# The last 64 rows of a first product: from stacked 128-row matmuls to pairs of 64-row matmuls

## The chip, the cores and the metric

The kernel runs on one core of a Trainium2 chip (trn2). The metric is device time in microseconds (us); the time before is the median of three runs. The engines that matter here are TensorE (PE for its matmuls, PEld for its weight loads), VectorE (DVE), ScalarE (ACT), GpSimd (POOL) and the DMA queue that SyncE issues (SP).

## The reference: what is computed

Input `x` is 8 x 4096 x 192, `weight_gen` is 8 x 4096 x 8 x 7; the weights `w_in` (192 x 2048) and `w_out` (2048 x 192) come as float64.

```python
w = softmax(weight_gen, axis=-1)                       # 7 taps per head
out[s, h] = sum over k of w[s, h, k] * x_pad[s + k, h]  # causal, 8 heads of 24 columns
h = out.reshape(32768, 192) @ w_in                     # first product, 192 rows deep
g = h * cos(h)
y = g @ w_out                                          # second product, 2048 rows deep
```

The result is 32768 x 192 in float32.

## The kernel before

**Tiling.** A block is 512 tokens (4 rows on each of 128 partitions); there are 64 blocks. In each block the 2048 columns of h are worked in 16 chunks of 128, two chunks at a time: 8 pairs per block, 512 pairs in all. The main loop (line 436) runs over the pairs; iteration i does the first product of pair i, the cosine chain of pair i and of pair i - 1, and the second product of a piece that lies 6 pairs back. Each engine issues in the order of the program, which is fixed at the end by lines 474 to 483.

**Precision.** Products that have to be as good as float32 are made of two parts, hi and lo, in the type float32r. Weights are split by `two_parts` (line 101), the tokens by `transposed` (line 253), which turns the mixed rows on TensorE (line 257) and splits them on ScalarE (`hi`, line 264) and VectorE (`lo`, line 265).

**First product, `ffn_in` (lines 274 to 284).** The product is 192 rows deep: 128 rows (the a parts) and the last 64 (the b parts). For each chunk five matmuls of 128 rows and 512 tokens are added up in one PSUM bank:

- wa_hi with a_lo, wa_lo with a_hi, wa_hi with a_hi for the 128 rows;
- wb with b_lo, wb with b_hi for the last 64. The tile `wb` holds the hi part of the 64 weight rows in partitions 0 to 63 and the lo part in 64 to 127, and b_hi and b_lo hold the same 64 rows of tokens twice, once in each half. So one matmul gives w_hi * b + w_lo * b, and the two give all four partial products.

That is ten matmuls for a pair, each with its own weights. The tile `h` is two PSUM banks, one for each chunk; there are three such tiles. A pair's h goes ACT `turn` (line 292), DVE fraction (296), ACT sine (300), DVE `g` (303), ACT `ghi` (309), DVE `glo` (313); after that its `h` tile is free for pair i + 3.

**Second product, `ffn_out` (lines 318 to 355).** Eight matmuls of 384 columns in float32r (line 329), then eight of 192 columns in bfloat16 (line 332), then ACT evicts (335).

So TensorE's sequence in most iterations is: ten matmuls of line 282, eight of line 329, eight of line 332, and round again. At pairs 5 and 6 of a block four transposes (line 257) come between lines 282 and 329.

**Preparation of the last 64 weight rows, `w_in_b` (lines 139 to 152).** It loads the raw words of two column ranges into the two halves of a tile, splits them into a temporary tile `parts`, and then copies `parts` into `wb` with four DMAs on the SP queue (line 150), so that hi and lo of one chunk lie one above the other. It is called twice; the first call covers pairs 0, 1, 4 and 5, the second pairs 2, 3, 6 and 7.

**Other work.** POOL mixes the tokens of later blocks (lines 225 to 245). Every four blocks a softmax batch runs, with three steps on DVE (lines 179, 188 to 189, 191).

Of the kernel before, what the change touches and what calls it, by code (L numbers as in the profile page):

```python
# [11 lines left out]
F32 = mybir.dt.float32  # L12
F32R = mybir.dt.float32r
I32 = mybir.dt.int32
# [6 lines left out]
P = 128  # L21
# [7 lines left out]
    return float(v)  # L29


# sin(SIN_SCALE * f + SIN_BIAS) = cos(2 pi f) for -3/4 <= f <= 1/4; both constants are a few ulp
# below 2 pi and pi / 2, so that the argument stays within the table's [-pi, pi].
SIN_SCALE = _below(TWO_PI, 2)
SIN_BIAS = _below(math.pi / 2, 1)

# The upper word of 2.0 ** -127 in float64, read as a float32: smaller values become denormal.
F64_SMALL = float(np.array([2.0 ** -127]).view(np.float32)[1])


# [1 line left out]
def tile_softmax_conv_then_cos_ffn(  # L42
# [8 lines left out]
    nc = tc.nc  # L51

    B, S, D = x.shape
    H, K = weight_gen.shape[2], weight_gen.shape[3]
    G = D // H
    NT = B * S
    F = w_in.shape[1]
    NFC = F // P
    RPP = NT // P          # tokens of one partition, in a row
    R = 4                  # tokens of a partition in one block  # L60
    NB = RPP // R          # blocks
    CT = R * P             # tokens of a block
    PAD = K - 1
    D2 = D - P             # 64
    RW = 16                # tokens of a partition in one softmax batch
    SB = RW // R           # blocks of one softmax batch
    NPAIR = NFC // 2       # pairs of f chunks in a block
    HALF = NPAIR // 2
    LAG = 6                # pairs from the first product to the second
    TR = 5                 # the pair at which the next block is transposed  # L70
    TMP = 6
    CW = 512               # weights of a partition that are converted at once

    const = ctx.enter_context(tc.tile_pool(name="const", bufs=1))
    gpool = ctx.enter_context(tc.tile_pool(name="gpool", bufs=9))
# [1 line left out]
    ps_h = ctx.enter_context(tc.tile_pool(name="ps_h", bufs=3, space=bass.MemoryType.PSUM))  # L77
    ps_m = ctx.enter_context(tc.tile_pool(name="ps_m", bufs=2, space=bass.MemoryType.PSUM))

    # partition q * B + n holds the tokens q * RPP.. of batch n  # L80
    x_v = x.rearrange("n (q r) d -> q n (r d)", r=RPP)
    g_v = weight_gen.rearrange("n (q r) h k -> q n (r h k)", r=RPP)
    o_v = out.rearrange("(n q r) d -> q n (r d)", n=B, r=RPP)
# [3 lines left out]
    nc.gpsimd.memset(early, 0.0)  # L87
    make_identity(nc, ident)

# [1 line left out]
    wa_hi = const.tile([P, F], F32R, name="wa_hi")  # L91
    wa_lo = const.tile([P, F], F32R, name="wa_lo")
    wb = const.tile([P, F], F32R, name="wb")   # rows 0-63 the first part, 64-127 the second
    wo = const.tile([P, NFC, 2 * D], F32R, name="wo")
    wo_b = const.tile([P, NFC, D], BF16, name="wo_b")

# [4 lines left out]
    def two_parts(raw, hi, lo, half=None):  # L101
        shape = hi.shape[1:]
        n = math.prod(shape)

        def shaped(t, steps=1):
            t = t.rearrange("p (n s) -> p n s", s=steps)
            return t if len(shape) == 1 else t.rearrange("p (a b) s -> p a b s", b=shape[1])

        low, top = (shaped(raw, 2)[..., k] for k in range(2))
        t1 = work.tile([P, 2, CW], F32, name="t1", tag="turn", bufs=TMP)  # L110
        size, bits = (shaped(t1.bitcast(I32)[:, k, 0:n])[..., 0] for k in range(2))
        nc.scalar.activation(out=size.bitcast(F32), in_=top.bitcast(F32), func=AF.Abs)
        yield
        nc.vector.tensor_scalar(  # L114
            out=size.bitcast(F32), in0=size.bitcast(F32), scalar1=F64_SMALL, scalar2=None, op0=ALU.max)
        yield
        nc.vector.tensor_scalar(
            out=size, in0=size, scalar1=0x07FFFFFF, scalar2=3,
            op0=ALU.bitwise_and, op1=ALU.logical_shift_left)
        yield  # L120
        # sign, exponent and 20 bits of the mantissa
        nc.vector.scalar_tensor_tensor(
            out=size, in0=top, scalar=-0x40000000, in1=size, op0=ALU.bitwise_and, op1=ALU.bitwise_or)
        yield
        # 3 more bits of the mantissa
        nc.vector.scalar_tensor_tensor(
            out=bits, in0=low, scalar=29, in1=size, op0=ALU.logical_shift_right, op1=ALU.bitwise_or)
        nc.scalar.copy(out=hi, in_=bits.bitcast(F32))  # L128
        if half is not None:
            nc.scalar.copy(out=half, in_=bits.bitcast(F32))  # L130
        yield
        nc.gpsimd.tensor_tensor(out=lo, in0=bits.bitcast(F32), in1=hi.bitcast(F32), op=ALU.subtract)  # L132

    def w_in_a(c0, c1):
        raw = words(c1 - c0)
        nc.sync.dma_start(out=raw, in_=w_in[0:P, c0:c1].bitcast(I32))
        return two_parts(raw, wa_hi[:, c0:c1], wa_lo[:, c0:c1])

    def w_in_b(j):
        raw = words(CW)  # L140
        cols = [slice(n * (F // 2) + j * CW, n * (F // 2) + (j + 1) * CW) for n in range(2)]
        for n in range(2):
            nc.sync.dma_start(out=raw[n * D2:(n + 1) * D2], in_=w_in[P:D, cols[n]].bitcast(I32))

        def convert():
            parts = gpool.tile([P, 2, CW], F32R, name="parts", tag="ghi")
            yield from two_parts(raw, parts[:, 0, :], parts[:, 1, :])
            for n in range(2):
                for m in range(2):
                    nc.sync.dma_start(out=wb.bitcast(F32)[m * D2:(m + 1) * D2, cols[n]],  # L150
                                        in_=parts.bitcast(F32)[n * D2:(n + 1) * D2, m, :])
        return convert()

    w_out_v = w_out.rearrange("(c p) d -> p c d", p=P)

# [4 lines left out]
        cs = slice(2 * q, 2 * q + 2)  # L160
        return two_parts(raw, wo[:, cs, 0:D], wo[:, cs, D:2 * D], wo_b[:, cs, :])

# [1 line left out]
    taps, ready = {}, set()  # L164

    def softmax(r0, r1, eng):
# [27 lines left out]
            out=t, in0=t, in1=den.unsqueeze(2).broadcast_to([P, n, K]), op=ALU.mult)  # L194
        ready.update(range(r0 // R, r1 // R))

# [1 line left out]
    rows, mixed = {}, {}  # L198

    def load_rows(b):  # L200
# [13 lines left out]
    def attention(b, eng, ra=0, rb=R, spare=False):  # L214
        xt = rows[b]
        t = taps[b]
        n = rb - ra
        # the columns from D on repeat the last D2, for both halves of the transposed rows
        if b not in mixed:
            xa_ = work.tile([P, R, D + D2], F32, name="xa")  # L220
            mixed[b] = xa_
        xa = mixed[b]

        def product(k, dst):
            eng.tensor_tensor(  # L225
                out=dst.rearrange("p r (h g) -> p r h g", h=H),
                in0=xt[:, k + ra:k + rb, :].rearrange("p r (h g) -> p r h g", h=H),
                in1=t[:, ra:rb, :, k:k + 1].broadcast_to([P, n, H, G]), op=ALU.mult)

        product(0, xa[:, ra:rb, 0:D])  # L230
        yield
        old = None
        for k in range(1, K + 1):
            if k < K:
                if spare:
                    pr = work.tile([P, R, D], F32, name="pr", tag="turn", bufs=TMP)
                else:
                    pr = work.tile([P, R, D], F32, name="pr", bufs=3)
                product(k, pr[:, ra:rb])
                yield  # L240
            if old is not None:
                if k == K:
                    eng.tensor_tensor(out=xa[:, ra:rb, D:], in0=xa[:, ra:rb, P:D],
                                      in1=old[:, ra:rb, P:D], op=ALU.add)
                eng.tensor_tensor(out=xa[:, ra:rb, 0:D], in0=xa[:, ra:rb, 0:D], in1=old[:, ra:rb],  # L245
                                  op=ALU.add)
                yield
            old = pr

# [1 line left out]
    xT = {}  # L251

    def transposed(b, part):
# [14 lines left out]

        return split

# [1 line left out]
    hs, g_parts = {}, {}  # L272

    def ffn_in(i):
        b, pair = divmod(i, NPAIR)
        a_hi, a_lo, b_hi, b_lo = xT[b]
        h = ps_h.tile([P, 2, CT], F32, name="h")
        for n in range(2):
            fs = slice((2 * pair + n) * P, (2 * pair + n + 1) * P)
            prods = ((wa_hi, a_lo), (wa_lo, a_hi), (wb, b_lo), (wb, b_hi), (wa_hi, a_hi))  # L280
            for m, (w, v) in enumerate(prods):
                nc.tensor.matmul(h[:, n, :], lhsT=w[:, fs], rhs=v,  # L282
                                 start=(m == 0), stop=(m == len(prods) - 1))
        hs[i] = h

# [1 line left out]
    turns = {}  # L287

    def act_turns(i):
# [22 lines left out]
        hi, lo = g_parts[i]  # L312
        nc.vector.tensor_tensor(out=lo, in0=hs.pop(i), in1=hi.bitcast(F32), op=ALU.subtract)  # L313

# [1 line left out]
    sums, finals = {}, {}  # L316

    def ffn_out(j):
# [47 lines left out]
            yield  # L366

    mixing = {1}
# [1 line left out]
    def all_of(*steps):  # L370
        steps = list(steps)
        while steps:
# [55 lines left out]
    for _ in range(4):  # L428
        next(bg)
    all_of(a1, b1)  # L430
# [1 line left out]
    N = NB * NPAIR  # L432

    sm = sm2
    no_split = split = lambda: None
    for i in range(N + LAG):
        b, pair = divmod(i, NPAIR)
# [33 lines left out]
            if (b if pair <= TR + 1 else b + 1) + 3 not in mixing:  # L471
                next(bg, None)

    # each engine issues in the order of this program
    issued = {}
    for ins in nc.cur_bb.bb.instructions:
        if ins.engine in issued:
# [11 lines left out]


def _as_sent(a):
    """float64 has no type on the chip: its words are sent as they are."""
    a = np.ascontiguousarray(a)
    return a.view(np.int64) if a.dtype == np.float64 else a

# [18 lines left out]
```

## Time and profile before

| | us |
|---|---|
| median of three runs | 2418.97 |
| lowest and highest of the three | 2418.47 and 2419.04 |
| span of the profiled execution, first to last instruction | 2416.5 |
| PE busy | 2345.7 |
| PEld busy | 2019.7 |
| DVE busy | 2037.1 |
| ACT busy | 1848.9 |
| POOL busy | 1877.6 |

The profile gives no time for its execution beyond the span; the span is 2.5 us below the median of the runs. Start times in the timeline count from the span's start. Matmuls overlap each other in the pipeline, so the time that one more matmul takes is read from the distance of two starts and not from the duration of one. In a timeline row the columns are start, duration, engine, line, operation, output and inputs, then rows x columns of the array for a matmul, the shape, and the number of merged instructions; a bracket gives the idle time before it and what ended it. The mean granted TensorE clock of the execution is 0.992 of full speed.

### The profile page before, as it was taken

To read this page: it belongs to the slowest core of one execution; us is meant where nothing else is said; L and a number is where in the kernel's file an instruction comes from. 1 tells how busy PE (TensorE), PEld (TensorE's weight loads), DVE (VectorE), ACT (ScalarE), POOL (GpSimd) and SP (SyncE) were. 2 spreads that over 40 slices of the span, in tenths; PEclk is the share of its full clock that TensorE was granted. 3 is DMA by queue.
4 is the path that set the end of the run, shared out by engine and by line. 5 is a ranking of instruction groups with operands and counts; after the bars stand their busy time and mean duration, and the time that the engine had idled before them with its cause. 6 is when DMAs were issued, how large, how long until landed. Compare 5 with 4: busy or idle time off the path is not lost.

```text
span 2416.5 us, 34582 instructions
## 1 busy us (share of the span) xinstructions
PE 2345.7 (97%) x13824; PEld 2019.7 (84%) x13824; DVE 2037.1 (84%) x1820; ACT 1848.9 (77%) x2266; POOL 1877.6 (78%) x1458
## 2 busy tenths in 40 slices
PE   2799999999999999999999999999999999999999
PEld 1588888888888888888888888888888888888888
DVE  8988888888888888888888888888888888888887
ACT  3678777787877778777787777878777787777876
POOL 6698878797787787787787787877877877887841
PEclk8899999999999999999999999999999999999999
DMA  6211220210211120121211211111111201201100
GB/s 163 53 42 36 47 54 24 54 47 23 54 47 31 46 54 24 47 51 27 54 37 33 54 35 43 47 27 51 46 31 47 54 24 46 54 24 48 30 7 20
DMA packets 25456, 104.93 MB, mean 43 GB/s; under 512 B 2782, under 2 KB 5462, under 8 KB 25294
## 3 DMA queue, kind: packets, MB, share of 16 engines
q1 hardware_dynamic: 25294, 102.72, 17.1%
q8 instruction: 108, 1.77, 0.3%
q14 instruction: 54, 0.44, 0.1%
HBM read 76.50 MB, written 25.17 MB: 42 GB/s over the span
## 4 chain that ended last, share of the span: by engine, by line
PE 87%; DVE 6%; ACT 5%; issue 1%; DMA 0%; SPq 0%; ACTq 0%; DVEq 0%
PE h L282 46%; PE ps_m L329 27%; PE ps_m L332 13%; PE ps_m L257 2%; ACT ghi L309 1%; ACT turn L292 1%; DVE h L303 1%; DVE glo L313 1%; DVE den L189 1%; ACT L300 1%; DVE turn L296 1%; ACT turn L300 1%; DVE t L114 1%; ACT L184 1%; DVE den L188 1%
## 5 line engine op out<-in xcount | busy, mean ns | idle before, releaser
L296 DVE TENSOR_TENSOR turn<-h,turn 128x1024 f32<-128x1024 f32 x512 | 625.5, 1222 | 326.3 <-ACT turn L292 323.3
L329 PE MATMUL ps_m<-wo,ghi 128*128 128x384 f32 x4096 | 812.9, 340 | 3.1 <-ACT part L335 3.1
L292 ACT ACTIVATE turn<-h 128x1024 int32<-128x1024 f32 x512 | 524.7, 1025 | 314.3 <-PE h L282 314.3
L329 PEld LDWEIGHTS ps_m<-wo,ghi 128*128 128x128 f32 x4096 | 721.1, 188 | 38.3 <-ACT part L335 3.6
L245 POOL TENSOR_TENSOR xa<-xa,pr 128x768 f32<-128x768 f32 (+1 forms) x384 | 705.4, 1837 | 5.0
L300 ACT ACTIVATE turn<-turn 128x1024 f32<-128x1024 f32 x512 | 543.4, 1061 | 184.2 <-DVE turn L296 184.0
L303 DVE TENSOR_TENSOR h<-h,turn 128x1024 f32<-128x1024 f32 x512 | 629.9, 1230 | 8.3 <-ACT turn L300 8.3
L313 DVE TENSOR_TENSOR glo<-h,ghi 128x1024 bf16<-128x1024 f32 x512 | 621.7, 1214 | 1.1 <-ACT ghi L309 1.1
L225 POOL TENSOR_TENSOR pr<-xt,taps 128x768 f32<-128x768 f32 (+1 forms) x384 | 588.2, 1537 | 0.0
L346 POOL TENSOR_TENSOR part<-part,part 128x384 f32<-128x384 f32 x252 | 256.3, 1017 | 391.2 <-ACT part L335 391.1
L309 ACT CAST ghi<-h 128x1024 fp32r<-128x1024 f32 x512 | 516.3, 1008 | 3.8 <-DVE h L303 2.8
L282 PE MATMUL h<-a_lo,wa_hi 128*128 128x512 f32 x1024 | 454.3, 444 | 33.2 <-DVE glo L313 25.5
L332 PE MATMUL ps_m<-wo_b,glo 128*128 128x192 bf16 x4096 | 426.8, 247 | 0.0
L282 PE MATMUL h<-a_hi,wa_hi 128*128 128x512 f32 x1024 | 408.0, 398 | 0.0
L282 PE MATMUL h<-a_hi,wa_lo 128*128 128x512 f32 x1024 | 406.8, 397 | 1.1 <-POOL wa_lo L132 1.1
L282 PE MATMUL h<-b_hi,wb 128*128 128x512 f32 x1024 | 404.6, 395 | 0.0
L282 PE MATMUL h<-b_lo,wb 128*128 128x512 f32 x1024 | 403.6, 394 | 0.8 <-DVE b_lo L265 0.8
L332 PEld LDWEIGHTS <-glo 128*128 128x128 bf16 x4096 | 311.7, 98 | 82.1 <-issue 82.1
L282 PEld LDWEIGHTS h<-a_lo,wa_hi 128*128 128x128 f32 x1024 | 194.7, 190 | 62.6 <-ACT wa_hi L128 13.6
L335 ACT ACTIVATE part<-ps_m 128x384 f32<-128x384 f32 x512 | 241.4, 472 | 6.8 <-PE ps_m L332 6.8
L282 PEld LDWEIGHTS h<-b_lo,wb 128*128 128x128 f32 x1024 | 194.2, 190 | 48.9 <-DVE b_lo L265 1.3
L282 PEld LDWEIGHTS h<-b_hi,wb 128*128 128x128 f32 x1024 | 194.2, 190 | 45.5
(52 smaller groups left out, 1285.6 us busy)
## 6 DMA issues: line engine op xcount, KB each, us to landing
xt<-in_x_dram SPq DMA_DIRECT2D x62, 960.0 KB, 7.4
out_dram<-fin SPq DMA_DIRECT2D x63, 384.0 KB, 3.9
taps<-in_weight_gen_dram SPq DMA_DIRECT2D x15, 448.0 KB, 8.6
raw<-in_moe_w_out_dram SPq DMA_DIRECT2D x8, 384.0 KB, 3.9
raw<-in_moe_w_in_dram SPq DMA_DIRECT2D x6, 256.0 KB, 6.6
raw<-in_moe_w_in_dram SPq DMA_DIRECT2D x3, 512.0 KB, 5.9
wb<-parts SPq DMA_DIRECT2D x8, 128.0 KB, 4.8
xt<-in_x_dram SPq DMA_DIRECT2D x1, 768.0 KB, 11.7
```

The source lines that it names most:

```text
L225: eng.tensor_tensor(out=dst.rearrange("p r (h g) -> p r h g", h=H), in0=xt[:, k + ra:k + rb, :].rearrange("p r (h g) -> p r h g", h=H), in ...
L245: eng.tensor_tensor(out=xa[:, ra:rb, 0:D], in0=xa[:, ra:rb, 0:D], in1=old[:, ra:rb], op=ALU.add)
L282: nc.tensor.matmul(h[:, n, :], lhsT=w[:, fs], rhs=v, start=(m == 0), stop=(m == len(prods) - 1))
L292: nc.scalar.activation(out=t.bitcast(I32), in_=hs[i], func=AF.Identity, bias=0.25, scale=1.0)
L296: nc.vector.tensor_tensor(out=t, in0=hs[i], in1=t.bitcast(I32), op=ALU.subtract)
L300: nc.scalar.activation(out=t, in_=t, func=AF.Sin, bias=SIN_BIAS, scale=SIN_SCALE)
L303: nc.vector.tensor_tensor(out=hs[i], in0=hs[i], in1=turns.pop(i), op=ALU.mult)
L309: nc.scalar.copy(out=hi, in_=hs[i])
L313: nc.vector.tensor_tensor(out=lo, in0=hs.pop(i), in1=hi.bitcast(F32), op=ALU.subtract)
L329: nc.tensor.matmul(acc[:, 0:2 * D], lhsT=g, rhs=wo[:, fc, :], start=(c == 0), stop=False)
L332: nc.tensor.matmul(acc[:, 0:D], lhsT=g, rhs=wo_b[:, fc, :], start=False, stop=(c == 2 * HALF - 1))
L346: eng.tensor_tensor(out=part, in0=part, in1=old, op=ALU.add)
```

## The change

The last 64 rows are no longer stacked. `wb` is replaced by `wb_hi` and `wb_lo`, each 128 x 1024: partitions 0 to 63 hold the 64 weight rows of the even chunks, partitions 64 to 127 those of the odd ones. In `ffn_in` each pair begins with six matmuls of 64 rows: three products (hi * lo, lo * hi, hi * hi; the product lo * lo is left out), and of each one matmul for the even chunk on partitions 0 to 63 and one for the odd chunk on partitions 64 to 127. They alternate between the halves and write to different PSUM banks. Six matmuls of 128 rows follow for the a parts. A pair has twelve matmuls and twelve weight loads in place of ten and ten.

`w_in_b` loads the raw words of the even chunks into the upper half and of the odd chunks into the lower, in runs of 128 weights (1 KB), and splits them straight into `wb_hi` and `wb_lo`. The temporary tile `parts` and the eight DMAs of line 150 are gone. Its first call now covers pairs 0 to 3 and the second pairs 4 to 7. The rest of the diff takes out comments.

```diff
-    wb = const.tile([P, F], F32R, name="wb")   # rows 0-63 the first part, 64-127 the second
+    wb_hi = const.tile([P, F // 2], F32R, name="wb_hi")
+    wb_lo = const.tile([P, F // 2], F32R, name="wb_lo")
...
+    w_in_odd_even = w_in.rearrange("k (a n c) -> n k a c", n=2, c=P)
+
     def w_in_b(j):
         raw = words(CW)
-        cols = [slice(n * (F // 2) + j * CW, n * (F // 2) + (j + 1) * CW) for n in range(2)]
+        pairs = slice(j * CW // P, (j + 1) * CW // P)
         for n in range(2):
-            nc.sync.dma_start(out=raw[n * D2:(n + 1) * D2], in_=w_in[P:D, cols[n]].bitcast(I32))
-
-        def convert():
-            parts = gpool.tile([P, 2, CW], F32R, name="parts", tag="ghi")
-            yield from two_parts(raw, parts[:, 0, :], parts[:, 1, :])
-            for n in range(2):
-                for m in range(2):
-                    nc.sync.dma_start(out=wb.bitcast(F32)[m * D2:(m + 1) * D2, cols[n]],
-                                        in_=parts.bitcast(F32)[n * D2:(n + 1) * D2, m, :])
-        return convert()
+            nc.sync.dma_start(out=raw[n * D2:(n + 1) * D2].rearrange("k (a c) -> k a c", c=2 * P),
+                              in_=w_in_odd_even[n, P:D, pairs, :].bitcast(I32))
+        cols = slice(j * CW, (j + 1) * CW)
+        return two_parts(raw, wb_hi[:, cols], wb_lo[:, cols])
...
         h = ps_h.tile([P, 2, CT], F32, name="h")
+
+        for m, (w, v) in enumerate(((wb_hi, b_lo), (wb_lo, b_hi), (wb_hi, b_hi))):
+            for n in range(2):
+                rs = slice(n * D2, (n + 1) * D2)
+                nc.tensor.matmul(h[:, n, :], lhsT=w[rs, pair * P:(pair + 1) * P], rhs=v[rs, :],
+                                 start=(m == 0), stop=False)
+
         for n in range(2):
             fs = slice((2 * pair + n) * P, (2 * pair + n + 1) * P)
-            prods = ((wa_hi, a_lo), (wa_lo, a_hi), (wb, b_lo), (wb, b_hi), (wa_hi, a_hi))
-            for m, (w, v) in enumerate(prods):
-                nc.tensor.matmul(h[:, n, :], lhsT=w[:, fs], rhs=v,
-                                 start=(m == 0), stop=(m == len(prods) - 1))
+            for m, (w, v) in enumerate(((wa_hi, a_lo), (wa_lo, a_hi), (wa_hi, a_hi))):
+                nc.tensor.matmul(h[:, n, :], lhsT=w[:, fs], rhs=v, start=False, stop=(m == 2))
         hs[i] = h
```

## The prediction

> **What bounds the kernel now.** I read the page first: busy shares, then the chain that ended last.
>
> ```profile
> span 2416.5 us, 34582 instructions
> ## 1 busy us (share of the span) xinstructions
> PE 2345.7 (97%) x13824; PEld 2019.7 (84%) x13824; DVE 2037.1 (84%) x1820; ACT 1848.9 (77%) x2266; POOL 1877.6 (78%) x1458
> ...
> PE 87%; DVE 6%; ACT 5%; issue 1%; DMA 0%; SPq 0%; ACTq 0%; DVEq 0%
> ```
>
> TensorE carries 87% of the chain. A busy PE need not be a PE at its limit, so I asked for the waits: ACT's first step waits for the h of TensorE, 409 times, while TensorE waits for a free h tile only 17 times.
>
> ```profile
> PE h L282 <- DVE glo L313: 25.5, 17, 6.8
> ...
> ACT turn L292 <- PE h L282: 314.3, 409, 1.4
> ```
>
> The window over four blocks (32 pairs) in the middle gives the rates that the other engines would allow. Its columns are the length, then the busy time of PE, PEld, DVE, ACT and POOL, then the granted clock, the DMA share and GB/s.
>
> ```profile
> 1382.24:1528.50 146.26, 145.52 (x865) 125.68 (x865) 123.67 (x109) 114.35 (x140) 117.19 (x90) 1.00 0.17 42
> ```
>
> A pair takes 146.26 / 32 = 4.57 us. PE idles 0.74 us in the whole window. DVE needs 123.67 / 32 = 3.86 us a pair, so 0.7 us a pair can go before DVE is the bound; ACT and POOL need less. The clock is 1.00. So what a pair costs TensorE is what the kernel costs, and the question is how long the new sequence is. The timeline of one ordinary pair:
>
> ```profile
> 1202.59 0.61 PEld L332 LDWEIGHTS <-glo 128*128 128x128 bf16 x8 [0.16 <-issue]
> 1202.60 0.83 PE L332 MATMUL ps_m<-wo_b,glo 128*128 128x192 bf16 x8
> ...
> 1203.19 0.19 PEld L282 LDWEIGHTS h<-a_lo,wa_hi 128*128 128x128 f32 x1
> 1203.21 0.48 PE L282 MATMUL h<-a_lo,wa_hi 128*128 128x512 f32 x1
> 1203.30 0.19 PEld L282 LDWEIGHTS h<-a_hi,wa_lo 128*128 128x128 f32 x1
> 1203.53 0.39 PE L282 MATMUL h<-a_hi,wa_lo 128*128 128x512 f32 x1
> 1203.53 0.19 PEld L282 LDWEIGHTS h<-b_lo,wb 128*128 128x128 f32 x1
> 1203.76 0.39 PE L282 MATMUL h<-b_lo,wb 128*128 128x512 f32 x1
> ...
> 1205.39 0.40 PE L282 MATMUL h<-a_hi,wa_hi 128*128 128x512 f32 x1
> ...
> 1205.62 1.57 PE L329 MATMUL ps_m<-wo,ghi 128*128 128x384 f32 x8
> ...
> 1207.03 0.83 PE L332 MATMUL ps_m<-wo_b,glo 128*128 128x192 bf16 x8
> ```
>
> Four things are read here. **A matmul of 512 tokens costs 0.2325 us**: from 1203.53 to 1205.39 lie eight steps, 1.86 / 8. Its duration of 0.39 to 0.40 is longer by 0.16, the time that it is still in the pipeline when the next has begun. **Its weights are loaded under the matmul before**: each load starts with that matmul. **A weight load holds the path for 0.11 us**: the loads at 1203.19 and 1203.30 start 0.11 apart though each is shown as 0.19 long. **The turn from line 332 costs little**: the second matmul starts at 1203.53, so the first streams from 1203.53 - 0.2325 = 1203.30, which is when its weights are in; its shown start at 1203.21 is early.
>
> **The change, part by part: TensorE.** Per pair four matmuls of line 282 go, two with b_lo and two with b_hi; the page counts 1024 of each form for the 512 pairs.
>
> ```profile
> L282 PE MATMUL h<-b_hi,wb 128*128 128x512 f32 x1024 | 404.6, 395 | 0.0
> L282 PE MATMUL h<-b_lo,wb 128*128 128x512 f32 x1024 | 403.6, 394 | 0.8 <-DVE b_lo L265 0.8
> ```
>
> Removed: 4 x 0.2325 = 0.93 us a pair. Added: six matmuls of 64 rows and 512 tokens, three on each half. No matmul in the trace has 64 rows, so the second of each two is bounded from both sides: it costs nothing where it runs wholly beside the first, and 0.2325 where it runs after it. From the code the two share no array row, no partition of the moving tile and no PSUM bank. They share the path of the weight loads. For a 64-row load I take the 0.11 of the 128-row one, the nearest row. Two loads, 0.22, fit under one matmul of 0.2325, so from the second product on the two halves can run side by side, with the lower half 0.11 behind the upper. The lag is paid once a pair, where the first two loads come one after the other behind the last matmul of line 332: upper half 1203.30, lower half 1203.41. Three steps from there end at 1203.41 + 3 x 0.2325 = 1204.11; the four matmuls of before would end at 1203.30 + 0.93 = 1204.23. **Saved: 0.12 us a pair, x 512 = 63 us.** The ends are 0.2325 x 512 = 119 saved (no lag) and 2 x 0.2325 x 512 = 238 lost (one after the other).
>
> This assumes that going from 128 rows to 64 and back costs nothing in itself, and the trace has no such turn. The nearest one is between products and transposes:
>
> ```profile
> 1218.69 0.39 PE L282 MATMUL h<-a_hi,wa_hi 128*128 128x512 f32 x1
> 1218.92 0.60 PE L257 MATMUL ps_m<-ident,xa 128*128 128x128 f32 x4
> 1219.27 1.64 PE L329 MATMUL ps_m<-wo,ghi 128*128 128x384 f32 x8
> 1220.76 0.83 PE L332 MATMUL ps_m<-wo_b,glo 128*128 128x192 bf16 x8
> ...
> L257 PE MATMUL ps_m<-ident,xa x512: 270/272/445, 27.6 to 2356.8; 128*128 128x128 f32 x171
> ```
>
> The transposes begin 0.23 after the matmul before, the usual step. They follow each other by (0.60 - 0.27) / 3 = 0.11, which is again one weight load each. From 1218.92 to 1220.76 are 1.84 us: four transposes (0.44) and eight matmuls of line 329 (1207.03 - 1205.62 = 1.41) are 1.85. So a change of operation empties no pipeline here, and I take 0 for the turn too, with 0.16 twice a pair as the other end (the third rival).
>
> **DVE's bursts.** Behind a softmax batch DVE has extra work within six pairs:
>
> ```profile
> 1214.87 1.08 DVE L179 TENSOR_REDUCE top<-taps 128x128 f32<-128x896 f32 x1
> ...
> 1221.64 0.69 DVE L265 SCALAR_TENSOR_TENSOR a_lo<-ps_m,a_hi 128x512 fp32r<-128x512 f32 x1 [0.18 <-ACT a_hi L264]
> ...
> 1227.54 0.69 DVE L265 SCALAR_TENSOR_TENSOR b_lo<-ps_m,b_hi 128x512 fp32r<-128x512 f32 x1 [0.18 <-ACT b_hi L264]
> ...
> 1231.05 1.08 DVE L188 TENSOR_REDUCE den<-taps 128x128 f32<-128x896 f32 x1
> 1232.16 1.53 DVE L189 TENSOR_SCALAR den<-den 128x128 f32<-128x128 f32 x1
> ...
> 1237.09 0.94 DVE L191 RECIPROCAL den<-den 128x128 f32<-128x128 f32 x1
> ```
>
> That is 6.0 us on six pairs, and the 0.74 us of PE idle time in the window belongs to it: PE runs out of h tiles there already. In the burst a faster PE gains nothing more: up to 6 x 0.12 = 0.7 us of the saving is lost each time, 0 if the three h tiles cover it. With some 15 batches that is 0 to 11 us; I take 0.45 each, 7 us.
>
> In later blocks the b parts come first now, which costs nothing: b_lo of the next block is done at 1227.54 + 0.69 = 1228.23, behind pair 6, and is first used at pair 8, a whole pair later.
>
> **The start.** Eight DMAs leave the SP queue:
>
> ```profile
> wb<-parts SPq DMA_DIRECT2D x8, 128.0 KB, 4.8
> ...
> 31.34 0.68 DVE L265 SCALAR_TENSOR_TENSOR b_lo<-ps_m,b_hi 128x512 fp32r<-128x512 f32 x1
> 31.48 0.80 PE L282 MATMUL h<-a_lo,wa_hi 128*128 128x512 f32 x1 [1.98 <-DVE a_lo L265]
> ...
> 40.50 0.79 PE L282 MATMUL h<-a_lo,wa_hi 128*128 128x512 f32 x1 [4.75 <-ACT wa_hi L128]
> ```
>
> Nothing waits for the copies now: the first matmul waited for a_lo and the second pair for wa_hi, so what goes was covered. Afterwards the first matmul needs b_lo, ready at 31.34 + 0.68 = 32.02 in place of 31.48: 0.5 us later. Against that the 64-row matmuls of the second pair need no new wa_hi and fit into the 4.75 us of waiting, worth about a microsecond. The raw words of `w_in_b` come in runs of 1 KB, and a late load would push the conversions behind it; I allow 3 us either way and count 0.
>
> **Sum.** -63 + 7 + 0 = -56 us on the span of 2416.5, which is 2.5 below the median; the same 2.5 lies around it afterwards. 2418.97 - 56 = **2363 us**.
>
> **The rivals.**
>
> *No lag between the halves* (chance 0.10). If the two loads go in together, the whole 119 us are saved, less 6 x 0.2325 = 1.4 us in each of 15 bursts (21): 2418.97 - 98 = 2321. For it: the halves share no row. Against it: the path of the loads is busy 84% of the span and never shows two starts closer than 0.11 in these rows. The Trainium skill, page "TensorE: Matmul & The Clock Gate", section "The mechanism", has packed matmuls of different row groups start about 4 ns apart; by that this rival would hold, and no run here shows it.
>
> *The halves run one after the other* (0.10). Then a pair has two matmuls more: +238, 2657. For it: every matmul of the trace starts one full step after the one before. Against it: none of them could do otherwise, since all use all rows.
>
> *The turn empties the array* (0.25), the one that ends slower. Place: between line 332 and the first 64-row matmul, and again before the first 128-row matmul. Price: what a matmul is still in the pipeline, 0.395 - 0.2325 = 0.16. The last matmul of line 332 ends at 1202.60 + 0.83 = 1203.43; by then the weights of both halves are in (1203.41), so both start at 1203.43, without lag; they stream to 1204.13 and are out at 1204.29, against 1204.23 before: +0.06 x 512 = +31, 2450. It decides from a turn of 0.12: 1203.41 + 0.6975 + 0.12 = 1204.23. Below that the change still gains. Against it: the transposes above. The Trainium skill, page "TensorEngine Tiling (Array Packing)", section "Key Properties", speaks for it: changing the tiling mode drains the engine. No turn of that kind is in the trace, and the page gives no price.
>
> *The turn also holds back the weight loads* (0.10). Then 0.11 for each half come behind 1203.43, the end moves to 1203.65 + 0.6975 + 0.16 = 1204.51, and the weights of the first 128-row matmul add 0.11: 1204.62, +0.39 x 512 = +200, 2619. Against it: the load at 1203.30 starts while line 332 is still in the array.
>
> **How the numbers follow.** Forecast 0.45, the two halves without lag 0.10, the emptying turn 0.25, the turn with loads 0.10, one after the other 0.10. The range of 2310 to 2480 takes in the first three and leaves out the last two, 0.20. The forecast's own range is 2340 to 2390. A measurement of this kernel can tell about 0.2% (4.8 us) from no change. Faster: 0.45 + 0.10 + 0.06 for a turn below 0.12 us; within 0.2%: 0.04, a turn near it; slower: 0.15 + 0.20.
>
> **What would show it.** In the timeline of the changed kernel the rows of 64-row matmuls should come in twos, the second within 0.11 us of the first, and the twos 0.23 apart; a step of 0.23 between all of them shows the halves one after the other. A first 128-row matmul more than 0.24 behind the last 64-row one shows an emptying turn; a weight load that starts only after it shows the last rival. From one group of line 332 to the next an ordinary pair should take 4.31 us in place of 4.43 (line 332 starts at 1202.60 and again at 1207.03). The wait of line 282 for glo should rise from 25.5 us by up to 11. The forecast is wrong if the weight loads of 64 rows take another time than those of 128, or if PE waits for glo in ordinary pairs.

## The result, and the profile after

| | median us | span of the profiled execution | PE clock |
|---|---|---|---|
| before | 2419.01 | 2416.5 | 0.992 |
| after | 2475.72 | 2473.9 | 0.993 |

The change makes the kernel slower: a ratio of 1.0234, 95% interval 1.0219 to 1.0248, 56.7 us. The forecast was 56 us faster. The line numbers shift: the 64-row matmuls are line 280 of the changed kernel, the 128-row ones of the first product line 286, the second product lines 332 and 335.

The page of the changed kernel, busy times and then the chain that ended last:

```profile
span 2473.9 us, 36612 instructions
## 1 busy us (share of the span) xinstructions
PE 2410.1 (97%) x14848; PEld 1888.1 (76%) x14848; DVE 2035.5 (82%) x1820; ACT 1849.6 (75%) x2266; POOL 1878.5 (76%) x1458
...
PE 95%; DVE 3%; ACT 1%; issue 1%; DMA 0%; POOL 0%; SPq 0%; ACTq 0%; DVEq 0%
```

TensorE still bounds it, even more than before: its share of the chain went from 87% to 95%. The busy times of DVE, ACT and POOL moved by less than 2 us; PEld fell by 132 us, though it has 1024 loads more. The window over four blocks, columns as in the prediction:

```profile
1200.00:1349.65 149.65, 149.65 (x929) 117.53 (x930) 123.36 (x109) 114.39 (x140) 117.23 (x90) 1.00 0.17 41
```

Four blocks take 149.65 us in place of 146.26, so 3.39 / 32 = 0.106 us more a pair, 54 us over 512 pairs. PE idles nowhere in this window. The 0.74 us that it waited in DVE's burst is gone: from 200 us on, PE waited for glo 12 times in the kernel before, 8.5 us in all, and once in the changed kernel, 0.5 us. Not every four blocks of the kernel before had such a wait, so 54 is a little less than the 56.7 us measured. So TensorE's own sequence became longer by 0.106 + 0.74 / 32 = 0.13 us a pair. The timeline of one ordinary pair, PE and PEld:

```profile
1202.75 0.61 PEld L335 LDWEIGHTS <-glo 128*128 128x128 bf16 x8 [0.16 <-issue]
1202.76 0.84 PE L335 MATMUL ps_m<-wo_b,glo 128*128 128x192 bf16 x8
1203.52 0.19 PEld L280 LDWEIGHTS h<-b_lo,wb_hi 64*128 64x128 f32 x2 [0.16 <-issue]
1203.52 0.50 PE L280 MATMUL h<-b_lo,wb_hi 64*128 64x512 f32 x2
1203.63 0.19 PEld L280 LDWEIGHTS h<-b_hi,wb_lo 64*128 64x128 f32 x2
...
1203.86 0.39 PE L280 MATMUL h<-b_hi,wb_lo 64*128 64x512 f32 x2
1203.86 0.19 PEld L280 LDWEIGHTS h<-b_hi,wb_hi 64*128 64x128 f32 x2
...
1204.09 0.40 PE L280 MATMUL h<-b_hi,wb_hi 64*128 64x512 f32 x2
1204.41 0.19 PEld L286 LDWEIGHTS h<-a_lo,wa_hi 128*128 128x128 f32 x1 [0.36 <-issue]
1204.42 0.50 PE L286 MATMUL h<-a_lo,wa_hi 128*128 128x512 f32 x1
1204.52 0.19 PEld L286 LDWEIGHTS h<-a_hi,wa_lo 128*128 128x128 f32 x1
1204.75 0.39 PE L286 MATMUL h<-a_hi,wa_lo 128*128 128x512 f32 x1
```

Two things are to be seen. **The 64-row matmuls do run in twos**: a row merges two (x2) and is 0.39 to 0.40 long, no longer than one matmul, and the twos are 0.23 apart. Even their weight loads come in twos, 0.19 for both. **The turns cost time** (a turn is a change between 128-row and 64-row matmuls): no weight load starts while the last 64-row matmuls stream. They start at 1204.09 and stream for 0.2325, to 1204.32; the next load starts at 1204.41, the matmul that needs it streams from 1204.75 - 0.2325 = 1204.52. The load at 1203.86, between 64-row matmuls, starts together with the matmul ahead of it.

That gives the price of each turn:

- **Back to 128 rows:** 1204.52 - 1204.09 = 0.43 where a step is 0.2325, so 0.20. Some 0.09 of it lies between the end of streaming and the load, 0.11 is the load.
- **To 64 rows:** the last matmul of line 335 starts at 1202.76 + 0.84 - 0.25 (its mean duration) = 1203.35, the first 64-row ones stream from 1203.86 - 0.2325 = 1203.63: 0.28, where before it was 1203.30 - 1203.18 = 0.12. So 0.16 more.

Together 0.36 a pair against one step of 0.2325 saved: +0.13, and the pair takes 4.55 us (1207.31 - 1202.76, the next start of line 335) where it took 4.43.

The groups of the 64-row matmuls, with busy time, mean ns and idle time before:

```profile
L280 PE MATMUL h<-b_lo,wb_hi 64*128 64x512 f32 x1024 | 257.5, 500 | 23.0 <-DVE glo L316 19.1 <-DVE b_lo L263 3.9
L280 PE MATMUL h<-b_hi,wb_hi 64*128 64x512 f32 x1024 | 204.7, 396 | 0.0
L280 PE MATMUL h<-b_hi,wb_lo 64*128 64x512 f32 x1024 | 202.0, 391 | 0.0
```

Busy time counts overlapping instructions once: 204.7 / 512 = 0.400 us for two matmuls that last 0.396 each. On the mean of the run the two halves start within 4 ns of each other.

### The profile page after: what moved, and what is told of

The parts are those of the page before. It is cut to its first block, busy times and chain, and to the rows that moved or that the text cites. A ratio compares the mean times of both kernels' runs of the same rounds, so it can differ in the third digit from the quotient of the medians.

```text
span 2473.9 us, 36612 instructions
## 1 busy us (share of the span) xinstructions
PE 2410.1 (97%) x14848; PEld 1888.1 (76%) x14848; DVE 2035.5 (82%) x1820; ACT 1849.6 (75%) x2266; POOL 1878.5 (76%) x1458
## 4 chain that ended last, share of the span: by engine, by line
PE 95%; DVE 3%; ACT 1%; issue 1%; DMA 0%; POOL 0%; SPq 0%; ACTq 0%; DVEq 0%
PE h L286 32%; PE ps_m L332 29%; PE h L280 18%; PE ps_m L335 14%; PE ps_m L255 2%; DVE t L116 1%; DVE glo L316 0%; DVE t L124 0%; DVE h L306 0%; DVE t L128 0%; DVE pr L223 0%; ACT ghi L312 0%; DVE xa L243 0%; DMA raw<-in_moe_w_in_dram 0%; ACT t L114 0%
## 5 line engine op out<-in xcount | busy, mean ns | idle before, releaser
L286 PE MATMUL h<-a_lo,wa_hi 128*128 128x512 f32 x1024 | 461.6, 451 | 3.7 <-ACT wa_hi L130 3.7
L280 PE MATMUL h<-b_lo,wb_hi 64*128 64x512 f32 x1024 | 257.5, 500 | 23.0 <-DVE glo L316 19.1
L286 PEld LDWEIGHTS h<-a_hi,wa_hi 128*128 128x128 f32 x1024 | 194.1, 190 | 46.4
L286 PEld LDWEIGHTS h<-a_hi,wa_lo 128*128 128x128 f32 x1024 | 195.3, 191 | 24.6 <-POOL wa_lo L134 1.8
L280 PE MATMUL h<-b_hi,wb_hi 64*128 64x512 f32 x1024 | 204.7, 396 | 0.0
```

What stands on the lines that cost most here:

```text
L280: nc.tensor.matmul(h[:, n, :], lhsT=w[rs, pair * P:(pair + 1) * P], rhs=v[rs, :], start=(m == 0), stop=False)
L286: nc.tensor.matmul(h[:, n, :], lhsT=w[:, fs], rhs=v, start=False, stop=(m == 2))
```

## The experiments

All are timed against the kernel before, 2419 us. The theory after the result: each turn between 128-row and 64-row matmuls lets the array run empty and holds back the next weights, some 0.2 us each. The main rival: twelve matmuls and twelve loads a pair are too many for TensorE's sequencer, for the profile puts the gaps down to "issue".

**1. Four turns a pair (four_turns).** The edit, on the changed kernel (`pack` and `whole` are its two loops, by product and by chunk):

```diff
-        for m, (w, v) in enumerate(((wb_hi, b_lo), (wb_lo, b_hi), (wb_hi, b_hi))):
...
-        for n in range(2):
-            fs = slice((2 * pair + n) * P, (2 * pair + n + 1) * P)
...
+        pack(0)
+        whole(0, False)
+        pack(1)
+        pack(2, True)
+        whole(1, True)
```

> The same twelve matmuls of a pair, but the 64-row ones are split in two groups (one product, then three 128-row matmuls of the even chunk, then two products, then the odd chunk), so a pair turns between 128 and 64 rows four times and not twice. Theory (each turn empties the array and holds back the next weight loads, about 0.20 us): two more turns a pair, 0.40 x 512 = +205 over the changed kernel, about 2680. Rival (two more instructions of each kind a pair are too many for the sequencer, the turn costs nothing): same instructions, so no change, about 2476. Rival (only the place behind the bfloat16 matmuls is dear): about 2476 too.

Measured: 2671.84 us, ratio 1.1044 (1.1028 to 1.1061), 196 us over the changed kernel, 0.38 us a pair for two more turns. The instructions are the same, only in another order, so the sequencer rival falls. PEld and PE at the added turn to 64 rows:

```profile
1204.15 0.19 PEld L287 LDWEIGHTS h<-a_hi,wa_hi 128*128 128x128 f32 x1
1204.71 0.18 PEld L281 LDWEIGHTS h<-b_hi,wb_lo 64*128 64x128 f32 x2 [0.37 <-issue]
```
```profile
1204.38 0.40 PE L287 MATMUL h<-a_hi,wa_hi 128*128 128x512 f32 x1
1204.71 0.50 PE L281 MATMUL h<-b_hi,wb_lo 64*128 64x512 f32 x2
1205.04 0.40 PE L281 MATMUL h<-b_hi,wb_hi 64*128 64x512 f32 x2
```

Behind a 512-column matmul too the load starts 0.33 after that matmul's start, 0.10 after its streaming, and not with it. So the rival that only the place behind the bfloat16 matmuls is dear falls too.

**2. Twelve matmuls without a turn (full_rows).** Every chunk's sum here also holds the other chunk's product.

```diff
-                rs = slice(n * D2, (n + 1) * D2)
-                nc.tensor.matmul(h[:, n, :], lhsT=w[rs, pair * P:(pair + 1) * P], rhs=v[rs, :],
+                nc.tensor.matmul(h[:, n, :], lhsT=w[:, pair * P:(pair + 1) * P], rhs=v,
```

> The six 64-row matmuls of a pair are made 128 rows deep (both halves of the same tiles, so the sum of each chunk also holds the other chunk's product): twelve matmuls and twelve loads a pair, no turn at all. Theory (turn): two steps of 0.2325 more than before the change, +238, about 2657, and no gaps at the places of the turns. Rival (sequencer): the same gaps of 0.16 and 0.20 a pair as in the changed kernel on top of that, +0.36 x 512 = 184, about 2840.

Measured: 2637.83 us, ratio 1.0904 (1.0887 to 1.092). That is 19 us below the theory's number and far from 2840. Some 8 of the 19 are the waits in the bursts, which a slower PE no longer has; the rest was not traced. The rows:

```profile
1203.01 0.71 PE L279 MATMUL h<-b_lo,wb_hi 128*128 128x512 f32 x2
1203.56 0.62 PE L279 MATMUL h<-b_hi,wb_lo 128*128 128x512 f32 x2
1204.01 0.64 PE L279 MATMUL h<-b_hi,wb_hi 128*128 128x512 f32 x2
1204.49 0.40 PE L285 MATMUL h<-a_lo,wa_hi 128*128 128x512 f32 x1
1204.72 0.39 PE L285 MATMUL h<-a_hi,wa_lo 128*128 128x512 f32 x1
```

Two of 128 rows take 0.62 to 0.64 and two steps, and line 285 follows 0.48 behind the start of two: no gap. Twelve matmuls and twelve loads a pair are no difficulty; the gap comes with the change in the number of rows.

**3. All on one half (same_half).** The odd chunk gets the even chunk's weights for these rows.

```diff
-                rs = slice(n * D2, (n + 1) * D2)
+                rs = slice(0, D2)
```

> All six 64-row matmuls of a pair use the upper half (the odd chunk is given the even chunk's weights for these rows). The turns stay. Theory (two matmuls of 64 rows run together only because they lie on different halves of the array): three steps of 0.2325 a pair more than the changed kernel, +357, about 2833. Rival (a 64-row matmul simply takes half the time, wherever it lies): no change, about 2476.

Measured: 2809.24 us, ratio 1.1612 (1.1593 to 1.1632), 333 us over the changed kernel where the theory has 357.

```profile
L280 PE MATMUL h<-b_hi,wb_hi 64*128 64x512 f32 x1024 | 318.0, 390 | 0.0
```
```profile
1205.74 0.39 PE L280 MATMUL h<-b_hi,wb_hi 64*128 64x512 f32 x1
1206.06 0.50 PE L286 MATMUL h<-a_lo,wa_hi 128*128 128x512 f32 x1
```

318.0 / 512 = 0.62 us for two: 0.39 and one step of 0.23. A 64-row matmul takes as long as a 128-row one; what saves time is only that the other half works beside it. The turn back is there with one half alone: line 286 is shown 0.32 behind the last 64-row matmul (0.33 in the changed kernel), so the gap does not come from the two halves working together.

**4. The halves apart (halves_apart).** First the upper half's three, then the lower half's.

```diff
-        for m, (w, v) in enumerate(((wb_hi, b_lo), (wb_lo, b_hi), (wb_hi, b_hi))):
-            for n in range(2):
+        for n in range(2):
+            for m, (w, v) in enumerate(((wb_hi, b_lo), (wb_lo, b_hi), (wb_hi, b_hi))):
```

> The same twelve matmuls and the same two turns a pair, but the three of the upper half are issued first and then the three of the lower half. Theory (matmuls start in program order, so only neighbours of different halves run together): five steps in place of three, +2 x 0.2325 x 512 = +238 over the changed kernel, about 2714. Rival (each half takes its own next matmul as soon as it is free): no change, about 2476.

Measured: 2478.59 us, ratio 1.0247 (1.0229 to 1.0264), the changed kernel's time to within 3 us. The theory of program order fell:

```profile
1204.73 0.50 PE L280 MATMUL h<-b_lo,wb_hi 64*128 64x512 f32 x2
1205.07 0.39 PE L280 MATMUL h<-b_hi,wb_lo 64*128 64x512 f32 x2
1205.29 0.40 PE L280 MATMUL h<-b_hi,wb_hi 64*128 64x512 f32 x2
```
```profile
L280 PE MATMUL h<-b_lo,wb_hi 64*128 64x512 f32 x1024 | 260.7, 499 | 21.3 <-DVE glo L316 18.7 <-DVE b_lo L263 2.6
```

The lower half's first matmul, the fourth in the program, starts with the upper half's first: 260.7 / 512 = 0.509 us for two of 0.499. Each half takes its own next matmul, so here the order between the halves doesn't matter. The Trainium skill, page "TensorE: Matmul & The Clock Gate", section "The mechanism", says that matmuls start and end strictly in program order; for the starts these rows show otherwise.

**5. The 64-row matmuls last (b_last).** The loop of the products in 128 rows is moved ahead of the loop in 64 rows.

> The 64-row matmuls of a pair come behind its 128-row ones, so the turn to 64 rows lies behind a 512-column float32r matmul and the turn back lies ahead of line 329 in place of the 512-column one. Theory (any turn costs about 0.09 us to empty and 0.11 us for the next weights, whatever stands on either side): 0.40 a pair and the turn of the loads behind the bfloat16 matmuls is as before the change, (0.40 - 0.2325) x 512 = +86 against before, less up to 10 us of DVE bursts, about 2495 to 2505. Rival (the turn behind the bfloat16 matmuls is the dear one, 0.28 us from their last start to the first 64-row one): below the changed kernel, about 2440.

Measured: 2485.70 us, ratio 1.0276 (1.0261 to 1.0291); 9 us below the lower end of the theory, and above the changed kernel, so the rival falls.

```profile
1200.04 0.39 PE L280 MATMUL h<-a_hi,wa_hi 128*128 128x512 f32 x1
1200.35 0.50 PE L285 MATMUL h<-b_lo,wb_hi 64*128 64x512 f32 x2
1200.69 0.39 PE L285 MATMUL h<-b_hi,wb_lo 64*128 64x512 f32 x2
1200.92 0.39 PE L285 MATMUL h<-b_hi,wb_hi 64*128 64x512 f32 x2
1201.24 1.68 PE L332 MATMUL ps_m<-wo,ghi 128*128 128x384 f32 x8
1202.76 0.83 PE L335 MATMUL ps_m<-wo_b,glo 128*128 128x192 bf16 x8
```

To 64 rows: from 1200.04 to 1200.69 - 0.2325 = 1200.46 is 0.42, 0.19 over a step. Back: line 332 is shown at 1201.24, 0.32 behind the last 64-row matmuls and 0.09 over a step, and it now takes 1.52 in place of 1.41 to line 335, because its first load no longer lies under a matmul: 0.20 together. The turn costs much the same behind 512 float32r columns as behind 192 bfloat16 ones; in the changed kernel only 0.04 of it hid behind what the loads cost there before.

**6. One turn a pair (two_pairs), and what held it up.** The 64-row matmuls of an even pair and of the next go behind the even pair's 128-row ones (`pack` issues the six of one pair):

```diff
+        if even:
+            pack(i, h, False)
+            nxt_t = ps_h.tile([P, 2, CT], F32, name="h")
+            started[i + 1] = nxt_t
+            pack(i + 1, nxt_t, True)
```

> The 64-row matmuls of an even pair and of the odd pair behind it are issued together, behind the even pair's 128-row ones, so there are two turns for two pairs. Theory (turn, 0.20 each): for two pairs 2 x 0.2325 saved and 0.40 paid, -0.065 x 256 = -17 against before the change, about 2402, if the earlier need of the next h tile costs nothing; with it up to 0.7 us for two pairs more, so 2402 to 2560 and a wait of the 64-row matmuls for glo where it is above. Rival (sequencer): about 2476.

Measured: 2459.82 us (2451.68 to 2468.34), ratio 1.0168 (1.0142 to 1.0195). It is faster than the changed kernel in each of its four runs, which lie 17 us apart, and slower than the kernel before. That is the theory's case with a wait for glo. The waits of PE in a window of 142 us, and a shorter window around the wait:

```profile
PE h L287 <- DVE glo L330: 3.0, 1, 3.0
```
```profile
1398.00:1432.00 34.00, 31.01 (x179) 24.62 (x179) 26.91 (x25) 24.95 (x30) 23.95 (x18) 0.90 0.17 42
```

The next h tile is wanted earlier, and in DVE's burst it isn't free: one wait of 3 us in four blocks, and the granted clock of these 34 us is 0.90. In shorter windows it is 1.00 up to 1408, 0.93 to 1412 (the wait ends at 1412.1), 0.50 to 1416, 0.71 to 1420 and 1.00 again after that: the clock falls behind the wait. Over the run it is 0.973. Two edits of the softmax batch were tried against this, each with the kernel before as a control:

```diff
-        nc.vector.tensor_scalar_add(out=den, in0=den, scalar1=1e-9)
+        eng.tensor_scalar_add(out=den, in0=den, scalar1=1e-9)
...
-        if b % SB == SB - 1 and pair == SMP and b + 4 < NB:
+        if b % SB == SB - 1 and pair == 6 and b + 4 < NB:
```

> The kernel before the change with the softmax batch started at pair 6 and not 2, so that its DVE steps no longer fall on the pairs of the transposes, and with the addition of 1e-9 moved from DVE to POOL for the batches that POOL works on. A control for the next kernel. Theory: the 0.74 us of PE idle time in four blocks goes, 15 x 0.74 = 11 us, about 2408. Rival (the idle time comes from elsewhere): 2419.

> two_pairs with the same two edits of the softmax batch as before_late. Theory (two_pairs paid one turn less a pair but lost it to one wait of 3 us in four blocks for a free h tile in the softmax burst, and to the clock that fell behind that wait): without the burst the waits and the clock loss go, 17 us below before_late, about 2391. Rival (the earlier need of the next h tile stalls in ordinary pairs too): at 2419 or above.

Measured: before_late 2429.65 us, ratio 1.0044 (1.0029 to 1.0059); two_pairs_late 2427.15, ratio 1.0034 (1.0021 to 1.0047). Neither theory held. At pair 6 the batch costs the old kernel more: PE now waits 15 times for ACT's evictions, where it waited twice, 3.1 us in all, in the kernel before. (That the exp of the batch puts ACT behind, so that the PSUM tiles come free late, is my reading and was not tested alone.) In two_pairs_late the wait for glo in four blocks went from 3.0 us to 1.8.

```profile
PE ps_m L329 <- ACT part L335: 21.2, 15, 2.5
```

So next the first edit alone, and once more the batch at pair 4:

> The kernel before the change with one edit of the softmax batch: the addition of 1e-9 to den (1.53 us on DVE) goes to POOL for the batches that POOL works on; the batch stays at pair 2. A control. Theory: up to 0.74 us of PE idle time in four blocks goes, 2408 to 2419. Rival (that idle time is ACT's, as in before_late): 2419.

> two_pairs with that one edit. Theory (the wait of 3.0 us for a free h tile in each softmax burst is DVE's): 1.5 us less in each of 15 bursts and no loss of clock behind it, so about 2459.8 - 22 - 20 = 2418 and a clock of 0.99; a version below 2419 if the wait goes altogether. Rival (it is the two ACT table loads of the batch): above 2440.

> two_pairs_den with the batch started at pair 4 in place of 2, so that exp with its two table loads falls on pair 7 and the DVE steps on pairs 0 and 1, where there are no transposes. Theory (bursts and transposes together exhaust the h tiles): below two_pairs_den, down to 2402. Rival (the burst alone is enough): like two_pairs_late, 2427.

Measured: before_den **2406.73 us**, ratio 0.9951 (0.9936 to 0.9966); two_pairs_den 2412.89, ratio 0.9975 (0.9965 to 0.9986); two_pairs_den4 2428.07, ratio 1.0038 (1.0023 to 1.0053). before_den lies 1 us below its range, two_pairs_den 5 us below its theory's 2418 with the clock it named, 0.991. two_pairs_den4 has its rival's time, and its waits for glo are longer than at pair 2 (39.2 us in the run against 32.9), so its theory fell; why pair 4 is worse was not found. Moving one addition off DVE takes away the burst's wait from the old kernel, and more than half of it from two_pairs. Windows of 146.3 us, the length of four blocks before the change, of before_den and then two_pairs_den, and for each two starts of the same softmax step eight blocks apart:

```profile
1200.00:1346.26 146.26, 146.26 (x870) 126.46 (x869) 123.09 (x109) 115.32 (x141) 117.78 (x91) 1.00 0.17 42
```
```profile
1200.00:1346.30 146.30, 144.95 (x933) 117.73 (x932) 122.10 (x107) 115.14 (x140) 118.31 (x92) 1.00 0.17 42
```
```profile
193.84 1.07 DVE L179 TENSOR_REDUCE top<-taps 128x128 f32<-128x896 f32 x1
...
484.40 1.08 DVE L179 TENSOR_REDUCE top<-taps 128x128 f32<-128x896 f32 x1
```
```profile
192.95 1.07 DVE L177 TENSOR_REDUCE top<-taps 128x128 f32<-128x896 f32 x1
...
484.42 1.08 DVE L177 TENSOR_REDUCE top<-taps 128x128 f32<-128x896 f32 x1
```

Four blocks take 290.56 / 2 = 145.28 us in before_den and 291.47 / 2 = 145.73 in two_pairs_den. In before_den PE is never idle in the window; in two_pairs_den it is still idle for 1.35 us in four blocks. Without that wait two_pairs_den would take 144.38: its sequence is 0.90 us shorter, where the theory's 2 x 0.2325 - 0.40 = 0.065 for two pairs gives 16 x 0.065 = 1.04. So half the turns do make the packing pay, but the wait that comes with the earlier need of the h tile takes more than the gain; what is left, 0.45 us in four blocks, makes 7 us over the run, and two_pairs_den is 6 us slower than before_den. The best kernel of the study is the old stacked product with the addition on POOL, 0.5% faster than the kernel before.

## Why the prediction was wrong

- **TensorE bounds the kernel, and a pair's sequence is the time:** right. In the steady part PE is never idle and its pairs are 0.13 us longer.
- **The two halves run beside each other from different rows:** right, and better than priced. The lag of 0.11, drawn from one load path, does not exist: both loads go in at once, and the halves start within 4 ns of each other. So a full step of 0.2325 is saved, where the forecast had 0.12. Alone that would have been the first rival's 119 us.
- **"Going from 128 rows to 64 and back costs nothing in itself":** this step failed. It was taken from the transposes, which follow the products without a gap. But those use all 128 rows; their rows show that a change of operation is free and say nothing of a change of rows. The turns cost 0.16 and 0.20, 0.36 x 512 = 184 us, against 119 saved: 65 us slower. Off that go the 12 waits in the bursts, 8 us by their length or 12 by the 0.98 us that four blocks lost in before_den; that leaves 53 to 57, and 56.7 were measured. Experiments 1, 2 and 3 show that the turns are what costs: two more cost 196 us, and without any there is no gap.
- **The turns as rivals:** the mechanism that came is the last rival's, the turn that also holds back the loads, which had 0.10 and 2619. It was priced too high: the two halves' loads take one 0.11 and not two, and the array needs about 0.09 and not 0.16 until the next load starts. The price of 0.16 was the modelled end of a matmul; in four_turns the load begins 0.10 after the end of streaming. The emptying turn that ends slower, with 2450, was nearer in time but by a mechanism that the rows refuse: the weights were not loaded ahead. That 2475.72 lies within the wide range of 2310 to 2480 is therefore luck: its upper end was set for that rival, and the mechanism that came had been put outside it. The Trainium skill, page "TensorEngine Tiling (Array Packing)", section "Key Properties", says that a change of the tiling mode drains the engine. These traces agree; the price, which it leaves out, is about 0.2 us a turn here, half of it the load that no longer lies under a matmul.
- **DVE's bursts, 7 us lost:** wrong in sign, since PE became slower. The wait for glo was to rise from 25.5 us by up to 11 and fell to 19.1. There were also fewer of these waits than the 15 batches that the forecast counted: 12.
- **The start, 0 within 3 us:** within that; the softmax step of the eighth block comes 7.3 us later, and the 59 pairs up to it, at 0.13 each, make 7.7.

What is open: what the 0.09 us between the end of streaming and the next load consist of, how much of two_pairs_den's idle time another order of the h tiles could remove, and why the batch costs more at pairs 4 and 6 than at pair 2.

## What to carry to other kernels

Packing small matmuls onto halves of the array pays by the steps it saves between one turn and the next, less two turns of about 0.2 us: at 0.23 us a step it takes two saved steps before it gains anything, so gather the packed matmuls or leave the rows stacked. A free transition in a trace is evidence only for transitions of its own kind; look at what stays the same in it. And when a faster sequence needs a buffer earlier, look for the burst that fills the buffers: here one addition moved from DVE to POOL gained 12 us, and no form of the packing was faster than that kernel.

## What the runs showed of the hardware that was not expected

- Matmuls of different halves start out of program order: with the halves issued apart the time moved from 2475.72 to 2478.59 only, and the fourth matmul starts with the first.
- Two 64-row weight loads of different halves take one load's time (0.19 for x2), and a 64-row load holds its path as long as a 128-row one: in the changed kernel the next load starts 0.11 behind it (1203.52 and 1203.63), as between 128-row loads (1204.41 and 1204.52).
- One wait of 3 us of TensorE cost more than itself: the granted clock of the 34 us around it was 0.90, with 0.50 in the 4 us behind it, and over the run 0.973. Where the wait was 1.35 us (two_pairs_den), the window with it has a clock of 1.00 and the run 0.991.
